# A spectral filter with a gated MLP on one core: the filtered spectrum stored class by class, its sums over twenty short rows, and a new order of work

## Chip, cores and metric

The kernel runs on one core of a Trainium2 chip. The metric is device time in microseconds (us): the median of 3 runs before the change is 196.58 us (196.56 to 196.6). Durations below are those of one profiled execution, which took 196.57 us.

## What is computed

With S = 2048 and D = 640, in bfloat16:

```
xn  = layernorm(x)                                     # over the last axis, no scale
A   = irfft2( rfft2(xn) * (w_r + i*w_i) )              # (2048, 640) real <-> (2048, 321) complex
B   = ((xn @ w_gate) * (xn @ w_up)) @ w_down           # 640 -> 1536 -> 640
out = x + A + B
```

## The kernel before

Everything is written as some 960 tasks (`T(name, engine, cost, emit, reads, writes, ...)`). Dependencies follow from the declared reads and writes. `_PLAN` is a list of (task, engine, PSUM bank) made ahead of time by a planner from the tasks' costs in ns; `replay` takes it as it stands, so it fixes the order on every engine, which of two engines does an eviction, and the bank of each product. Each engine works through its list strictly in order and waits on semaphores. A task that takes a bank waits for the last eviction of the task that had the bank before. `hold` moves the other dependencies of an eviction to its product, so that PE, not the evicting engine, waits for them.

TensorE (PE) does all products. In order of time:

- Layernorm and the gate and up products. `T0` transposes the first blocks (L814), `xt` DMAs on the queue of SP the others. `GU_f_b_w` (L973 and L951) multiplies 128 columns f of w_gate or w_up with rows b; `eG` evicts it, and `H` (L991, L993) multiplies gate with up on the Vector engine (DVE).
- The row transform: `S1` to `S5` on DVE, `R` on PE (L905), `eR` evicts. The remaining gate and up products fill PE between all these.
- The filter stage, for t = 0 to 15. `D` (L1034, 10 products each) is the last part of the forward transform over the columns: 321 frequencies in five classes of equal remainder (four classes of 64, one of 65). `eD` evicts it. `C` (L1053) is the transform over the rows. `WM` (L1070 four times, L1073 once) multiplies C in PSUM with the filter's real and imaginary parts. `SM`, after every second WM, adds and subtracts the parts over two row halves (L1086, L1087) and writes the filtered spectrum `L`. `JA`, `JB` (1024 columns each, on DVE or ACT) and `JC`, `JD` (252 columns, on GpSimd, POOL) write the mirrored or negated parts beside it. `IA` (L1116) takes five stationary blocks of 128 columns from `L`, multiplies with 64 columns of a table, and `eIA` evicts.
- The inverse over the columns, `I` (L1144) with evictions `eI` and combinations `V1` to `V5` on DVE, beside the down product `ACC` (L1221). `IV` (L1233) adds the spectral part into the same bank, `FINA` and `FIN` evict and add x, and `st_out` stores.

The evictions and copies share the helper lines L681 (ACT) and L682 (DVE and POOL). In `L` a row of 640 columns belongs to one frequency row; before the change the four classes of 64 are interleaved in it, so that for four of the five blocks of an IA the columns lie 4 elements apart, and the sums write at an odd offset:

```
o_ = 640 * (q % 4)
yl = v_l[:, lr, o_ + 128 + k:o_ + 640:4] if k < 4 else v_l[:, lr, o_:o_ + 128]
```

The filter is read from three buffers in turn (`ld_w`, on the queue of SP), one buffer for two t; further loads there are `ld_gw` (w_gate, w_up), `ld_wd` (w_down), `ld_tf`, `ld_ti`, `ld_fd`, `ld_g`, `ld_sm1` (tables) and `ld_x`.

Of the kernel before, what the change touches and what calls it, by code (L numbers as in the profile page):

```python
# [255 lines left out]
def _build_tables():  # L256
    t = {}
# [7 lines left out]
    for tt in range(16):  # L265
        for g in range(_G):
            q = tt * _G + g
# [14 lines left out]
    b = np.arange(64)  # L282
# [18 lines left out]
    l_ = 5 * np.arange(65)  # L301
    e = np.exp(-1j * two_pi * ((b[:, None] * l_[None, :]) % _D) / _D)
    w = np.where((l_ == 0) | (l_ == 320), 1.0, 2.0)[:, None] / _D * np.conj(e).T
    for o in range(2):
        own = (l_ % 2 == o).astype(np.float64)
        fd[64 * o:64 * o + 64, 512:577] = e.real * own[None, :]
        fd[64 * o:64 * o + 64, 578:641] = (e.imag * own[None, :])[:, 1:64]
        gd[63:128, 512 + 64 * o:576 + 64 * o] = w.real * own[:, None]
        gd[0:63, 512 + 64 * o:576 + 64 * o] = -(w.imag * own[:, None])[1:64]
# [59 lines left out]
_LP = 321  # L369
_YS = 1090  # L370
# [30 lines left out]
def _d_act(n):  # L401
# [4 lines left out]
    (12, 1, -1), (19, 2, -1), (10, 0, 1), (0, 3, -1), (11, 4, -1), (13, 4, -1), (18, 2, -1), (20, 2, -1), (28, 2, -1),  # L406
    (27, 2, -1), (170, 1, -1), (14, 4, -1), (8, 3, -1), (21, 1, -1), (22, 2, -1), (29, 2, -1), (23, 2, -1), (30, 1, -1),
    (31, 2, -1), (32, 2, -1), (24, 0, 3), (25, 2, -1), (26, 2, -1), (9, 0, 7), (33, 0, 1), (34, 2, -1), (35, 2, -1),
    (181, 0, 0), (182, 2, -1), (36, 1, -1), (37, 1, -1), (15, 4, -1), (43, 1, -1), (38, 1, -1), (169, 4, -1), (179, 0, 6),
    (180, 2, -1), (39, 2, -1), (40, 2, -1), (183, 2, -1), (44, 1, -1), (45, 1, -1), (46, 2, -1), (47, 2, -1), (189, 0, 1),  # L410
    (191, 0, 0), (190, 1, -1), (192, 1, -1), (193, 2, -1), (172, 4, -1), (186, 0, 6), (171, 4, -1), (112, 2, -1), (187, 1, -1),
    (41, 0, 2), (42, 1, -1), (184, 0, 7), (185, 1, -1), (16, 4, -1), (54, 2, -1), (113, 2, -1), (48, 0, 6), (49, 1, -1),
    (62, 1, -1), (194, 0, 5), (196, 0, 3), (197, 1, -1), (195, 1, -1), (188, 2, -1), (198, 2, -1), (50, 2, -1), (51, 2, -1),
    (53, 2, -1), (114, 2, -1), (55, 2, -1), (52, 2, -1), (63, 1, -1), (206, 0, 2), (207, 1, -1), (64, 1, -1), (204, 0, 7),
    (205, 1, -1), (115, 2, -1), (173, 4, -1), (209, 0, 6), (174, 4, -1), (65, 1, -1), (210, 1, -1), (66, 1, -1), (67, 2, -1),
    (56, 1, -1), (57, 2, -1), (116, 2, -1), (199, 0, 3), (200, 1, -1), (70, 2, -1), (201, 0, 2), (202, 1, -1), (203, 2, -1),
    (58, 2, -1), (208, 2, -1), (17, 4, -1), (121, 2, -1), (72, 1, -1), (1, 4, -1), (211, 0, 7), (175, 4, -1), (212, 1, -1),
    (176, 4, -1), (177, 4, -1), (73, 1, -1), (117, 0, 2), (118, 1, -1), (119, 0, 5), (74, 1, -1), (213, 2, -1), (122, 2, -1),
    (68, 2, -1), (123, 2, -1), (75, 1, -1), (76, 1, -1), (77, 2, -1), (216, 0, 1), (217, 1, -1), (214, 0, 0), (215, 1, -1),
    (218, 2, -1), (221, 0, 2), (222, 1, -1), (78, 2, -1), (124, 2, -1), (219, 0, 3), (220, 1, -1), (223, 2, -1), (80, 2, -1),  # L420
    (224, 0, 4), (120, 1, -1), (225, 1, -1), (82, 1, -1), (60, 2, -1), (226, 0, 2), (227, 1, -1), (229, 0, 6), (230, 1, -1),
    (83, 1, -1), (84, 1, -1), (178, 4, -1), (231, 0, 5), (125, 2, -1), (128, 0, 6), (126, 0, 3), (129, 1, -1), (232, 1, -1),
    (228, 2, -1), (130, 2, -1), (233, 2, -1), (131, 2, -1), (59, 4, -1), (71, 4, -1), (2, 4, -1), (236, 0, 0), (237, 1, -1),
    (61, 4, -1), (85, 1, -1), (234, 0, 2), (127, 1, -1), (86, 1, -1), (235, 1, -1), (238, 2, -1), (132, 2, -1), (92, 1, -1),
    (241, 0, 6), (242, 1, -1), (239, 0, 7), (240, 1, -1), (93, 1, -1), (243, 2, -1), (133, 2, -1), (87, 2, -1), (246, 0, 4),
    (244, 0, 1), (245, 1, -1), (94, 1, -1), (247, 1, -1), (248, 2, -1), (134, 2, -1), (69, 4, -1), (249, 0, 6), (250, 1, -1),
    (95, 1, -1), (96, 1, -1), (97, 2, -1), (251, 0, 2), (252, 1, -1), (90, 2, -1), (253, 2, -1), (88, 2, -1), (98, 2, -1),
    (100, 2, -1), (254, 0, 7), (255, 1, -1), (256, 0, 3), (257, 1, -1), (438, 4, -1), (433, 4, -1), (259, 0, 4), (260, 1, -1),
    (258, 2, -1), (137, 0, 5), (139, 0, 0), (437, 4, -1), (435, 4, -1), (441, 4, -1), (472, 4, -1), (101, 4, -1), (91, 4, -1),
    (434, 4, -1), (470, 4, -1), (3, 4, -1), (135, 0, 2), (136, 1, -1), (143, 2, -1), (138, 1, -1), (102, 1, -1), (261, 0, 7),  # L430
    (262, 1, -1), (79, 4, -1), (89, 4, -1), (141, 0, 3), (269, 0, 2), (263, 2, -1), (142, 1, -1), (140, 1, -1), (266, 0, 5),
    (267, 1, -1), (144, 2, -1), (270, 1, -1), (264, 0, 4), (265, 1, -1), (268, 2, -1), (145, 2, -1), (271, 0, 5), (274, 0, 1),
    (103, 1, -1), (104, 1, -1), (272, 1, -1), (273, 2, -1), (81, 4, -1), (442, 4, -1), (466, 4, -1), (146, 2, -1), (105, 1, -1),
    (106, 1, -1), (275, 1, -1), (279, 0, 4), (280, 1, -1), (276, 0, 0), (277, 1, -1), (278, 2, -1), (107, 2, -1), (147, 2, -1),
    (110, 2, -1), (108, 2, -1), (468, 4, -1), (469, 4, -1), (281, 0, 6), (282, 1, -1), (286, 0, 7), (287, 1, -1), (283, 2, -1),
    (284, 0, 3), (152, 0, 4), (148, 0, 6), (153, 1, -1), (99, 4, -1), (431, 4, -1), (440, 4, -1), (432, 4, -1), (4, 4, -1),
    (683, 4, -1), (109, 4, -1), (111, 4, -1), (473, 4, -1), (156, 2, -1), (429, 4, -1), (439, 4, -1), (467, 4, -1), (471, 4, -1),
    (149, 1, -1), (285, 1, -1), (288, 2, -1), (157, 2, -1), (150, 0, 0), (289, 0, 2), (151, 1, -1), (154, 0, 4), (291, 0, 6),
    (296, 0, 0), (290, 1, -1), (292, 1, -1), (155, 1, -1), (293, 2, -1), (158, 2, -1), (301, 0, 2), (299, 0, 6), (300, 1, -1),
    (294, 0, 4), (295, 1, -1), (304, 0, 7), (306, 0, 6), (6, 4, -1), (297, 1, -1), (298, 2, -1), (159, 2, -1), (160, 2, -1),  # L440
    (305, 1, -1), (307, 1, -1), (309, 0, 0), (310, 1, -1), (302, 1, -1), (303, 2, -1), (311, 0, 7), (312, 2, -1), (308, 2, -1),
    (163, 0, 5), (164, 1, -1), (167, 0, 1), (161, 0, 3), (162, 1, -1), (168, 2, -1), (314, 0, 0), (315, 2, -1), (313, 2, -1),
    (165, 0, 4), (316, 0, 6), (317, 2, -1), (166, 1, -1), (446, 0, 2), (447, 1, -1), (448, 2, -1), (474, 0, 0), (443, 0, 4),
    (444, 2, -1), (445, 1, -1), (324, 0, 7), (325, 1, -1), (477, 0, 2), (479, 1, -1), (478, 2, -1), (318, 2, -1), (321, 0, 6),
    (322, 1, -1), (436, 4, -1), (451, 0, 4), (452, 2, -1), (475, 1, -1), (476, 1, -1), (449, 0, 2), (450, 2, -1), (498, 4, -1),
    (503, 4, -1), (504, 4, -1), (497, 4, -1), (534, 4, -1), (453, 2, -1), (319, 0, 7), (320, 1, -1), (323, 2, -1), (454, 2, -1),
    (326, 0, 6), (327, 1, -1), (328, 2, -1), (505, 0, 4), (506, 1, -1), (508, 0, 0), (509, 1, -1), (510, 1, -1), (331, 0, 7),
    (332, 1, -1), (334, 0, 2), (335, 1, -1), (329, 0, 6), (507, 1, -1), (482, 0, 0), (483, 2, -1), (480, 0, 2), (481, 2, -1),
    (484, 2, -1), (455, 1, -1), (330, 1, -1), (341, 0, 7), (342, 1, -1), (336, 0, 4), (337, 1, -1), (456, 3, -1), (457, 3, -1),
    (460, 0, 5), (462, 0, 6), (463, 1, -1), (458, 0, 0), (464, 0, 7), (465, 1, -1), (461, 1, -1), (344, 0, 1), (345, 1, -1),  # L450
    (536, 0, 6), (459, 1, -1), (537, 1, -1), (339, 0, 2), (538, 1, -1), (340, 1, -1), (349, 0, 1), (532, 4, -1), (500, 4, -1),
    (499, 4, -1), (502, 4, -1), (501, 4, -1), (511, 0, 3), (333, 2, -1), (485, 2, -1), (531, 4, -1), (565, 4, -1), (535, 4, -1),
    (560, 4, -1), (530, 4, -1), (528, 4, -1), (529, 4, -1), (513, 0, 6), (351, 0, 0), (486, 2, -1), (350, 1, -1), (352, 1, -1),
    (512, 2, -1), (567, 0, 1), (568, 1, -1), (569, 1, -1), (346, 0, 5), (347, 1, -1), (487, 3, -1), (488, 3, -1), (489, 0, 4),
    (490, 1, -1), (514, 2, -1), (338, 2, -1), (515, 2, -1), (354, 0, 0), (355, 1, -1), (539, 0, 2), (540, 1, -1), (541, 1, -1),
    (493, 0, 1), (491, 0, 6), (492, 1, -1), (494, 2, -1), (356, 0, 4), (357, 1, -1), (359, 0, 7), (360, 1, -1), (517, 2, -1),
    (343, 2, -1), (516, 2, -1), (495, 0, 2), (5, 4, -1), (430, 4, -1), (533, 4, -1), (544, 0, 0), (594, 4, -1), (561, 4, -1),
# [887 lines left out]
```

## Time and profile before

| What | Value |
|---|---|
| median of 3 runs | 196.58 us |
| the profiled execution | 196.57 us, its span 194.9 us |
| granted clock of PE | 1.00 |
| WM_1 starts, WM_15 ends | 72.73 us, 125.47 us |
| SM, two instructions | 823 ns each |
| JA, JB on DVE | 452 and 517 ns; on ACT 1056 ns |
| JC, JD on POOL | 510 and 943 ns |
| an eviction eD of 64x642 | DVE 826 ns, ACT 702 ns |
| an eviction eIA of 128x320 | DVE 486 ns, ACT 440 ns |

A group line of the profile gives line, engine, operation, the names and shapes of what is written and read, and a count; then busy time in us and the mean of one in ns; then the engine's idle time ahead of it and what ended most of it. PE is the matmuls, PEld the loading of their stationary operand, which overlaps them. Neighbouring instructions of an engine overlap a little, so their durations add up to more than the time they take. The chain is followed back from the last instruction.

### The profile page before, as it was taken

Reading aid. Unit: us, or ns where it says so; the run is one execution under the profiler, and the core shown is the slowest. Engines: PE = TensorE matmul, PEld = TensorE weight load, DVE = VectorE, ACT = ScalarE, POOL = GpSimd, SP = SyncE. Lnnn points to the kernel's source line nnn. Section 1 sums busy time; section 2 is a strip of 40 time slices with the busy share of each in tenths; the row PEclk is TensorE's granted clock in tenths of the full one; section 3 lists DMA queues with packets and bytes.
Section 4 is the critical chain, followed back from the end, with each engine's and each line's share of the span. In section 5 each row is a group of like instructions: output and inputs, shape, how many; then the busy total and the mean of one; then the engine's idle time right before and its main releaser. Section 6 shows DMA issues by size and latency. Waiting matters only on the chain.

```text
span 194.9 us, 4074 instructions
## 1 busy us (share of the span) xinstructions
PE 190.9 (98%) x1568; PEld 120.5 (62%) x1568; DVE 176.7 (91%) x369; ACT 136.4 (70%) x275; POOL 12.2 (6%) x22
## 2 busy tenths in 40 slices
PE   8899999999999999999999999999999999999995
PEld 8797454454454565555655555557777777777774
DVE  3899999999999999999989999987999999999713
ACT  3899999999884679989999999667305523253130
POOL 1000000000000000331031221120000000000000
DMA  5999974016869921366465510005001543135412
GB/s 173 324 370 324 214 98 111 0 37 105 155 130 222 258 68 27 96 145 193 118 153 135 153 36 31 3 0 170 4 0 53 144 143 104 40 95 172 134 68 67
DMA packets 29666, 23.73 MB, mean 122 GB/s; under 512 B 10448, under 2 KB 27600, under 8 KB 29520
## 3 DMA queue, kind: packets, MB, share of 16 engines
q1 hardware_dynamic: 28848, 23.08, 46.5%
q10 hardware_dynamic: 800, 0.41, 0.7%
q8 instruction: 12, 0.20, 0.5%
q14 instruction: 6, 0.05, 0.1%
HBM read 18.89 MB, written 2.62 MB: 110 GB/s over the span
## 4 chain that ended last, share of the span: by engine, by line
PE 95%; DVE 2%; DMA 1%; ACT 1%; issue 0%
PE ps L951 48%; PE ps L1221 27%; PE ps L973 5%; PE ps L1116 3%; PE ps L1034 2%; PE ps L1053 2%; PE ps L905 2%; PE ps L1144 2%; PE ps L1233 2%; DMA arena<-in_A_x_dram 1%; DVE arena L754 1%; PE ps L814 1%; ACT arena L681 1%; DVE arena L682 0%; DVE arena L761 0%
## 5 line engine op out<-in xcount | busy, mean ns | idle before, releaser
L681 ACT ACTIVATE arena<-ps 128x512 bf16<-128x512 f32 (+5 forms) x211 | 111.3, 582 | 48.8 <-PE ps L1233 13.8
L951 PE MATMUL ps<-arena 128*128 128x512 bf16 x440 | 101.9, 379 | 0.0
L951 PEld LDWEIGHTS ps<-arena 128*128 128x128 bf16 x440 | 40.9, 98 | 43.1 <-ACT arena L681 0.9
L1221 PE MATMUL ps<-arena 128*128 128x320 bf16 (+2 forms) x396 | 57.2, 295 | 0.0
L1221 PEld LDWEIGHTS ps<-arena 128*128 128x128 bf16 x396 | 37.6, 98 | 13.2
L1070 DVE TENSOR_TENSOR arena<-ps,arena 128x256 bf16<-128x256 f32 x64 | 22.6, 414 | 1.5 <-PE ps L1053 1.3
L991 DVE TENSOR_TENSOR arena<-arena 128x512 bf16<-128x512 bf16 x44 | 18.7, 426 | 0.6 <-ACT arena L681 0.2
L1260 DVE TENSOR_TENSOR arena<-arena 128x640 bf16<-128x640 bf16 x15 | 7.0, 486 | 5.4 <-ACT arena L681 5.4
L682 DVE CAST arena<-ps 128x512 bf16<-128x512 f32 (+4 forms) x16 | 10.1, 639 | 1.5 <-PE ps L973 0.4
L745 ACT ACTIVATE arena<-arena 128x640 bf16<-128x640 bf16 x12 | 10.2, 849 | 0.1
L682 POOL COPY arena<-arena 64x252 bf16<-64x252 bf16 x8 | 4.1, 510 | 92.8 <-DVE arena L1087 92.5
L973 PE MATMUL ps<-arena 128*128 128x128 bf16 (+1 forms) x120 | 9.5, 237 | 0.3 <-DVE arena L682 0.3
L1116 PEld LDWEIGHTS ps<-arena 128*128 128x128 bf16 x160 | 7.9, 116 | 3.0
L736 ACT ACTIVATE arena<-arena 128x640 bf16<-128x640 bf16 x12 | 9.0, 753 | 0.2
L973 PEld LDWEIGHTS ps<-arena 128*128 128x128 bf16 x120 | 8.4, 98 | 1.1 <-issue 0.4
L1100 POOL TENSOR_SCALAR arena<-arena 64x252 bf16<-64x252 bf16 x8 | 7.5, 943 | 22.9 <-DVE arena L1087 22.6
L1116 PE MATMUL ps<-arena 128*128 128x64 bf16 x160 | 8.3, 198 | 0.0
L1233 PE MATMUL ps<-arena 128*128 128x320 bf16 (+2 forms) x33 | 8.3, 295 | 0.0
L1034 PEld LDWEIGHTS ps<-arena 128*128 128x128 bf16 x160 | 6.4, 98 | 2.7 <-issue 0.5
L857 DVE TENSOR_TENSOR arena<-arena 128x768 f32<-128x768 bf16 (+1 forms) x10 | 7.9, 789 | 0.0
L1073 DVE TENSOR_TENSOR arena<-ps,arena 128x260 bf16<-128x260 f32 x16 | 6.9, 432 | 0.0
L1034 PE MATMUL ps<-arena 128*128 128x64 bf16 (+1 forms) x160 | 6.9, 193 | 0.0
(61 smaller groups left out, 184.3 us busy)
## 6 DMA issues: line engine op xcount, KB each, us to landing
arena<-in_A_x_dram SPq DMA_DIRECT2D x19, 160.0 KB, 2.6
arena<-in_A_w_i_dram SPq DMA_DIRECT2D x30, 80.2 KB, 2.3
arena<-in_A_w_r_dram SPq DMA_DIRECT2D x30, 80.2 KB, 2.3
out_dram<-arena SPq DMA_DIRECT2D x15, 160.0 KB, 1.9
arena<-in_B_w_gate_dram SPq DMA_DIRECT2D x4, 320.0 KB, 6.5
arena<-in_A_x_dram SPq DMA_DIRECT2D x1, 1280.0 KB, 10.8
arena<-c_tf SPq DMA_DIRECT2D x4, 256.0 KB, 4.6
arena<-c_ti SPq DMA_DIRECT2D x2, 512.0 KB, 5.0
```

The costliest lines, as they stand in the source:

```text
L681: return c.e.activation(dst, src, _ACTF.Copy)
L682: return c.e.tensor_copy(dst, src)
L736: return c.e.activation(v_jk, v_x[:, b, :], _ACTF.Copy, scale=1.0 / _D, accum_out=v_m32[:, b:b + 1])
L745: return c.e.activation(v_jk, v_x[:, b, :], _ACTF.Square, scale=-1.0, bias=v_m32[:, b:b + 1], accum_out=v_ss[:, b:b + 1])
L951: ins = c.e.matmul(ps[:, bk, :], v_gw[:, w, j, ft, :], v_xt[:, j, rows], start=(j == 0), stop=(j == 4))
L973: ins = c.e.matmul(ps[:, bk, i * n:(i + 1) * n], v_gw[:, w, j, ft0 + i, :], v_xt[:, j, rows], start=(j == 0), stop=(j == 4))
L991: return c.e.tensor_tensor(v_ht[:, ft0, rows], gb[:, 0, :], gb[:, 1, :], _OP.mult)
L1034: ins = c.e.matmul(ps[:, bk + i, k * 64:k * 64 + n], v_uq[:, k, t + i, :], v_fd[:, k * 128 + w * n: k * 128 + w * n + n], start=True, stop ...
L1070: c.e.tensor_tensor(dst, xh, wv, _OP.mult)
L1116: ins = c.e.matmul(ps[:, bk, 64 * k:64 * k + 64], yl, v_ti[:, q, 0, :], start=True, stop=True)
L1221: ins = c.e.matmul(ps[:, bk, 0:sl3.stop - sl3.start], v_ht[:, ft, a * 128:(a + 1) * 128], v_wd[:, ft, sl3], start=(ft == _FT_ORDER[0]), st ...
L1233: return c.e.matmul(ps[:, bank_of(own), 0:sl3.stop - sl3.start], v_sm[:, 2, :], v_v[:, a, sl3], start=False, stop=True)
```

## The change

The spectrum `L` and the products `PR` ahead of it are stored class by class: block b of a row is the class of 65 (b = 0) or one of the four of 64, and a block is 128 columns in `L` and 66 in `PR`. All five stationary blocks of an IA are contiguous then. WM runs over the classes outside and their members inside: it reads PSUM contiguously, where it had read in steps of 64, and the filter in steps of 10, where it had read four neighbours at a time. SM works on twenty rows of 66 instead of one run of 1284 elements written as four rows of 321. A memset on POOL (`pad`) zeroes what is beyond a class's members. In JC and JD the destination moves behind the source (at 65), and the table `g` has its rows in the new order.

```diff
-        gd[63:128, 512 + 64 * o:576 + 64 * o] = w.real * own[:, None]
-        gd[0:63, 512 + 64 * o:576 + 64 * o] = -(w.imag * own[:, None])[1:64]
+        gd[0:65, 512 + 64 * o:576 + 64 * o] = w.real * own[:, None]
+        gd[65:128, 512 + 64 * o:576 + 64 * o] = -(w.imag * own[:, None])[1:64]
...
+_LB = 66
...
-        b_pr = alloc("PR", 8 * 321)
-        b_l = alloc("L", 2 * 2624)
+        b_pr = alloc("PR", 8 * 5 * _LB)
+        b_l = alloc("L", 2 * 2560)
...
-        v_pr = V("PR").rearrange("p (w g n) -> p w g n", w=2, g=4)
-        v_l = V("L").rearrange("p (r n) -> p r n", r=2)
+        v_pr = V("PR").rearrange("p (w g b c) -> p w g b c", w=2, g=4, b=5)
+        v_l = V("L").rearrange("p (r g b c) -> p r g b c", r=2, g=4, b=5)
...
-                        xh = ps[:, bk:bk + 2, 0:256].rearrange("p g (k h m) -> p h g m k", k=4, h=2)[:, h]
-                        wv = wt[:, w, :, 0:320].rearrange("p g (m k) -> p g m k", k=10)
-                        wv = wv[:, :, :, 1:5] if h == 0 else wv[:, :, :, 9:5:-1]
-                        dst = v_pr[:, w, 2 * pb:2 * pb + 2, 65:321].rearrange("p g (h m k) -> p h g m k", h=2, k=4)[:, h]
+                        xh = ps[:, bk:bk + 2, 0:256].rearrange("p g (k h m) -> p h g k m", k=4, h=2)[:, h]
+                        wv = wt[:, w, :, 0:320].rearrange("p g (m k) -> p g k m", k=10)
+                        wv = wv[:, :, 1:5] if h == 0 else wv[:, :, 9:5:-1]
+                        dst = v_pr[:, w, 2 * pb:2 * pb + 2, 1:5, 32 * h:32 * h + 32]
...
-                d5 = v_pr[:, :, 2 * pb:2 * pb + 2, 0:65]
+                d5 = v_pr[:, :, 2 * pb:2 * pb + 2, 0, 0:65]
...
-            wm = T("WM_%d" % t, "dve", 1792.0, em_wm,
+            if t == 0:
+                def em_pad(c):
+                    return c.e.memset(v_pr[:].rearrange("p w g b c -> p (w g b) c")[:, :, 64:_LB], 0.0)
+                T("pad", "pool", 300.0, em_pad, writes=[(b_pr, None)], prio=pq - 0.002)
+            wm = T("WM_%d" % t, "dve", 1710.0, em_wm,
...
-                pa_, pb_ = v_pr[:, 0], v_pr[:, 1]
-                l_ = v_l[:, lr, 63:2623].rearrange("p (g n) -> p g n", g=4)[:, :, 0:321]
+                pa_, pb_ = (v_pr[:, w].rearrange("p g b c -> p (g b) c") for w in range(2))
+                l_ = v_l[:, lr].rearrange("p g b c -> p (g b) c")[:, :, 0:_LB]
                 c.e.tensor_tensor(l_[0:64], pa_[0:64], pb_[64:128], _OP.subtract)
                 return c.e.tensor_tensor(l_[64:128], pa_[64:128], pb_[0:64], _OP.add)
-            T("SM_%d" % t, "dve", 1900.0, em_sm, reads=[(b_pr, ("r", 0, 2))],
+            T("SM_%d" % t, "dve", 1640.0, em_sm, reads=[(b_pr, ("r", 0, 2))],
...
-                src = l0[:, :, 1:64] if five else l0[:, :, 65:321]
-                dst = l1[:, :, 0:63] if five else l0[:, :, 321:577]
+                src = v_l[:, lr, :, 0, 1:64] if five else v_l[:, lr, :, 1:5, 0:64]
+                dst = v_l[:, lr, :, 0, 65:128] if five else v_l[:, lr, :, 1:5, 64:128]
...
-{"act": 1200.0, "dve": 460.0, "pool": 1300.0},
+{"act": 1000.0, "dve": 440.0, "pool": 1000.0 if neg else 560.0},
...
-                        yl = v_l[:, lr, o_ + 128 + k:o_ + 640:4] if k < 4 else v_l[:, lr, o_:o_ + 128]
+                        yl = v_l[:, lr, q % 4, (k + 1) % 5]
...
-                ia = T("IA_%d" % q, "pe", 173.0, em_ia,
+                ia = T("IA_%d" % q, "pe", 146.0, em_ia,
```

`_PLAN` is replaced as a whole. The tasks are the same but for `pad`. From ACT to DVE go eR_13, eG_3_8_0, eD_2_0_0, JB_1, eIA_5, eIA_8, eD_10_0_0, JB_7, eIA_22, JA_13, eIA_30 and eI_2; from DVE to ACT eG_0_8_1, eR_15, eD_2_1_0, eIA_6, JA_7, eG_3_12_0, eG_10_12_1, JB_15 and eIA_28. DVE's queue from WM_1 to WM_9, before and after:

```
before: WM_1 WM_0 SM_1 H_2_8 JA_1 H_3_8 WM_3 WM_2 SM_3 H_4_8 JA_3 JB_3 WM_4 WM_5 H_5_8 SM_5 eIA_6
        JB_5 H_6_8 JA_5 WM_6 WM_7 H_7_8 SM_7 JA_7 H_8_8 WM_9
after:  WM_1 WM_0 SM_1 H_1_8 JA_1 JB_1 WM_2 WM_3 H_2_8 SM_3 JA_3 JB_3 H_3_8 WM_4 WM_5 H_4_8 H_5_8 SM_5
        eIA_5 H_6_8 JB_5 JA_5 WM_6 WM_7 eIA_8 H_7_8 SM_7 eD_10_0_0 JB_7 H_8_8 WM_9
```

On PE, GU, D, C and IA change places by a few positions (IA_13 goes ahead of D_12_1, for one), and in the column stage the parts of ACC and IV do. D_12_1 takes the banks of C_9 in the new order, which WM_9 frees, and GU_8_12_1 one that WM_15 frees. On the queue of SP the loads ahead of 120 us are shuffled: ld_sm1 goes ahead of ld_x5, ld_gw6_1 behind ld_gw8_0, the transpose xt8 from place 32 to 40, ld_w2_0_0 and ld_w2_0_2 from 36 and 37 to 54 and 55, ld_wd7 from 44 to 79. On POOL some of the mirrors swap.

## Prediction

> **What bounds the kernel now.** I read the page's engine shares and chain first, then the groups by form, the waits, and the Vector engine's time line between 72 and 126 us.
>
> ```profile
> PE 190.9 (98%) x1568; PEld 120.5 (62%) x1568; DVE 176.7 (91%) x369; ACT 136.4 (70%) x275; POOL 12.2 (6%) x22
> ...
> PE 95%; DVE 2%; DMA 1%; ACT 1%; issue 0%
> ```
>
> TensorE is busy for 98% of the span and is 95% of the chain that ended last: whatever shortens or stops PE moves the end by as much. DVE at 91% is close behind. The stretches show where the two meet (columns: length, busy us of PE, PEld, DVE, ACT, POOL, clock, DMA share, GB/s):
>
> ```profile
> 72.70:104.20 31.50, 31.50 (x281) 17.36 (x280) 30.29 (x74) 29.84 (x53) 5.98 (x8) 1.00 0.49 125
> 104.20:125.50 21.30, 21.26 (x189) 11.78 (x187) 20.08 (x47) 20.40 (x39) 4.35 (x6) 1.00 0.24 65
> ```
>
> This is the filter stage, from WM_1 to WM_15. PE never stops, and DVE idles for only 1.2 of each 31.5 or 21.3 us. Part of that is 0.03 us between dependent instructions; the rest is waiting for the products C:
>
> ```profile
> DVE arena L1070 <- PE ps L1053: 1.3, 4, 0.4
> ```
>
> So DVE has little more than 1.3 us in hand over 53 us.
>
> **The weights of the inverse column products (IA, L1116), on PE.** The groups by form (busy us, mean ns):
>
> ```profile
> L1116 PE MATMUL ps<-arena 128*128 128x64 bf16 x160 | 8.3, 198 | 0.0
> L1116 PEld LDWEIGHTS ps<-arena 128*128 128x128 bf16 x160 | 7.9, 116 | 3.0
> L1034 PEld LDWEIGHTS ps<-arena 128*128 128x128 bf16 x160 | 6.4, 98 | 2.7 <-issue 0.5 <-ACT arena L681 0.2
> L1034 PE MATMUL ps<-arena 128*128 128x64 bf16 x128 | 6.5, 193 | 0.0
> ```
>
> and their pace in the chain (start, us, what):
>
> ```profile
> 69.05 0.89 PE ps L1034 x30
> ...
> 81.64 0.67 PE ps L1116 x20
> ```
>
> L1034 has the same shape with contiguous stationary columns: 0.89/30 = 29.7 ns each. L1116, of whose five weights four step by 4 elements, takes 0.67/20 = 33.5. Five at 29.5 are 147 ns instead of 168, and 32 groups save 32 x 21 = 0.66 us. A rule speaks against this: the Trainium skill, "TensorE: Matmul & The Clock Gate", section "Weight-path perf modes — Fast Weight Load (FWL) and DoubleRow", has 128 bf16 weights loaded fast from chunks that are packed or strided alike. By it the saving is 0. The rows differ by 18 ns per load and 4 ns of pace, so I take 0.66 and keep 0 for a rival.
>
> **The sums SM (L1086, L1087), on DVE.** 20 rows of 66 are 1320 elements instead of 1284. The same operation took 426 ns for 512 elements (L991) and 823 for 1284: 0.51 ns per element, so 36 more cost 19 ns, twice per SM, 0.3 us over eight. The Trainium skill, "VectorE: DVE Perf Modes", section "Mode 2×_1P — pack two bf16 into one 32-bit read", asks for 4-byte aligned operands. The old sums write at an odd element offset, so by that rule they ran one element a cycle and the aligned layout would save about 0.6 us in each of 16 instructions, 10 us of DVE. The 0.51 ns rate is already two per cycle, so I count no gain. What short rows cost at this rate no row shows: 0 to another 0.6 us per instruction if two per cycle were lost.
>
> **The weighting WM (L1070), on DVE.** The same 256 elements, now reading PSUM contiguously and the filter in steps of 10:
>
> ```profile
> L1070 DVE TENSOR_TENSOR arena<-ps,arena 128x256 bf16<-128x256 f32 x64 | 22.6, 414 | 1.5 <-PE ps L1053 1.3
> L1073 DVE TENSOR_TENSOR arena<-ps,arena 128x260 bf16<-128x260 f32 x16 | 6.9, 432 | 0.0
> L1242 DVE TENSOR_TENSOR arena<-ps,arena 128x320 bf16<-128x320 f32 x1 | 0.5, 492 | 0.6 <-PE ps L1233 0.6
> L1242 DVE TENSOR_TENSOR arena<-ps,arena 128x192 bf16<-128x192 f32 x1 | 0.4, 359 | 0.5 <-PE ps L1233 0.5
> ```
>
> Contiguous PSUM and contiguous second operand interpolate to 426 ns at 256 elements, so the strided read of 414 pays nothing that could be won back. L1073 already steps through the filter by 5 and lies 14 ns above what 256 elements would give it. I take 0; the bounds are -12 and +14 ns for each of 64, or -0.8 to +0.9 us.
>
> **Mirrors, pad, table.** JA and JB keep 1024 elements (452 and 517 ns on DVE, 1056 on ACT): 0, within 0.05 us each. JC and JD keep 252 on POOL, which is 6% busy; after SM_1 they have about 0.5 us before IA_3, and beyond that PE waits. The new memset has 80 elements: between the 97 ns of POOL's smallest memset and the 294 of its 128-element select. It can run once S5_4 is done (65.5 us) and is needed by WM_1 at 72.7; were it late, WM_1 would be late by as much. The inverse table keeps its shape. Zero for each.
>
> **The new order.** *Queue of SP.* Filter loads move among the transposes; the runs they need land 3 us or more ahead of their WM in the old trace, and where ld_w2 now queues behind ld_w4 (which waits for the last R, near 67.7) it lands near 72.3 for a WM at 77. xt8 lands near 59, needed at 63.3. ld_wd7 moves past 35 issues to near 90, with its use after 131. Only ld_gw6_1 becomes thin: behind the 0.65 MB of ld_gw8_0 it lands near 22.6 instead of 20.8, and PE asks at 22.7. I take 0, at most 0.2. ld_sm1 ahead of ld_x5 ends PE's 0.2 us wait for c_sm and delays sm8 on ACT by 0.2: even. *POOL* swaps mirrors only.
>
> *DVE.* Here I count. From the start of WM_1 to the end of WM_9 the new queue holds, beyond the old: H_1_8 (0.43), JB_1 (0.52), an inverse eviction eIA_8 (0.49), a forward eviction eD_10_0_0 (0.83), JB_7 for JA_7 (0.07), and 4 x 0.04 for the sums: 2.5 us, some 2.3 after the 0.08 us by which neighbours overlap. WM_1 cannot move: it follows C_1, which has the same work ahead of it on PE. The old stretch:
>
> ```profile
> 72.73 1.41 DVE L1070 TENSOR_TENSOR arena<-ps,arena 128x256 bf16<-128x256 f32 x4
> ...
> 100.74 1.42 DVE L1070 TENSOR_TENSOR arena<-ps,arena 128x256 bf16<-128x256 f32 x4 [0.42 <-PE ps L1053]
> 102.07 0.45 DVE L1073 TENSOR_TENSOR arena<-ps,arena 128x260 bf16<-128x260 f32 x1
> ```
>
> WM_9 ends at 102.52 with 0.62 us of waits before it (0.20 and this 0.42). With every wait refilled it ends at 102.5 - 0.6 + 2.3 = 104.2. D_12_1 takes the banks that WM_9 frees. It started at 103.3; 13 cheaper IA ahead of it (-0.27) and one more of them (+0.15) put it at 103.2. PE therefore stands at least 1.0 to 1.1 us. At WM_15 the count is alike, not added: 2.8 us more work, 1.5 us of waits, so 125.5 becomes 126.8, against GU_8_12_1 at 126.35 - 28 x 0.021 = 125.8: again 1.0. PE has no idle time later to take this back in. ACT gains some 3 us of room in the stage (six evictions and mirrors fewer, one eviction more), which shortens nothing: no PE wait there ends on ACT. The column stage follows, where IV_8_0 at 168.7 follows V5_8 by only 0.1 us; it also slips with PE, and DVE's further 0.2 us of waits and its 1 us wait before V1_0 can be refilled: nothing more.
>
> **Sum.** Against this execution's 196.57 us (span 194.9 and 1.67 around it, 0.01 below the median of 196.58): -0.66 for the weights, +1.05 for DVE if it never waits, +0.2 for waits that remain when C and WM take turns: +0.6, or 197.2 us.
>
> **Rivals.** *DVE keeps up (faster).* The mechanism is the handover WM_9 to D_12_1: if DVE does the stretch 1 us quicker than the rows add up to, PE never stands and 0.66 stays: 195.9. The deciding point for faster by over 0.2% (0.39 us, about what a measurement of this kernel can tell from no change) is a stall below 0.27 us, that is 45 WM instructions each about 18 ns shorter. For it: the diff's own cost of a WM falls from 1792 to 1710 and of an SM from 1900 to 1640. Against it: SM took 1.65 before, and the contiguous rows above leave 12 ns at best. *The weights save nothing:* 168 ns stays, the stall does too: 197.9. *Strided filter reads cost 14 ns:* 0.5 us more at WM_9, 0.9 at WM_15: 197.9. *Short rows end two per cycle:* 0.6 us x 16 on a full DVE: about 206.
>
> **Chances.** DVE-bound with 0.66 saved: 0.60 (own range 196.6 to 197.9, of which 0.15 falls within 0.2%). DVE keeps up: 0.22 (0.17 faster, 0.05 within). Strided filter 0.08, no saving 0.05, short rows 0.05, all slower. Faster 0.17, within 0.20, slower 0.63. The range 196.0 to 198.3 leaves out the short rows and the best of the second case.
>
> **What would show it.** Right: L1116's successor at 29.5 ns pace and 98 ns loads; PE gaps at D and GU ended by the weighting's last line, first near 103 us; DVE's waits for C mostly gone; SM near 842 ns, WM's parts near 414. Wrong: PE unbroken from 72 to 131 us; or WM parts below 400; or gaps placed in the column stage instead.

## Result: 6.6% slower, and DVE now sets the filter stage

The changed kernel takes 209.59 us (median of 5 runs, 209.4 to 209.75) against 196.59 for the kernel before on the same chip: a ratio of 1.0663, 95% interval 1.0647 to 1.0678. The profiled execution has a span of 208.0 us at a granted clock of 1.00. The prediction was 197.2 us, with a range that ended at 198.3.

The engine line and the chain's shares, from the page of the changed kernel:

```profile
PE 192.3 (92%) x1551; PEld 119.5 (57%) x1568; DVE 190.5 (92%) x372; ACT 136.5 (66%) x272; POOL 12.5 (6%) x23
...
PE 62%; DVE 34%; issue 2%; DMA 2%; SPq 0%; ACT 0%; DVEq 0%
```

PE had 95% of the chain and has 62%. DVE went from 2% to 34%, and its busy time rose by 13.8 us, about what the kernel lost. The groups by form show where (line numbers are one to five higher than before):

```profile
L1071 DVE TENSOR_TENSOR arena<-ps,arena 128x256 bf16<-128x256 f32 x64 | 34.9, 611 | 0.1
L1118 PE MATMUL ps<-arena 128*128 128x64 bf16 x160 | 8.3, 193 | 4.0 <-DVE arena L1074 3.6 <-POOL arena L683 0.3
L1074 DVE TENSOR_TENSOR arena<-ps,arena 128x260 bf16<-128x260 f32 x16 | 7.0, 440 | 0.0
L1118 PEld LDWEIGHTS ps<-arena 128*128 128x128 bf16 x160 | 6.8, 98 | 8.3 <-DVE arena L1074 4.9 <-issue 0.9 <-ACT arena L1102 0.4
L1091 DVE TENSOR_TENSOR arena<-arena 64x1320 bf16<-64x1320 bf16 x8 | 6.7, 842 | 0.3
L1092 DVE TENSOR_TENSOR arena<-arena 64x1320 bf16<-64x1320 bf16 x8 | 6.7, 840 | 0.1
```

The four parts of WM (L1071) take 611 ns each instead of 414. The loads of IA (L1118) fell from 116 to 98 ns and the sums came to 842, both as forecast. DVE idles 0.1 us ahead of all 64 parts; PE waits for WM's last line instead. These are the stretches from WM_1 to the end of WM_9 and from there to WM_15 (length; busy us of PE, PEld, DVE, ACT, POOL; clock; DMA share; GB/s), and three of PE's waits (us in total, times, longest):

```profile
73.12:111.18 38.06, 31.87 (x268) 16.59 (x271) 37.38 (x73) 28.94 (x51) 5.80 (x8) 1.00 0.44 117
111.18:139.42 28.24, 23.49 (x204) 12.47 (x207) 27.71 (x53) 20.80 (x38) 4.58 (x6) 1.00 0.25 68
```

```profile
PE ps L1118 <- DVE arena L1074: 3.6, 5, 1.0
PE ps L952 <- DVE arena L1074: 3.4, 5, 1.0
PE ps L1035 <- DVE arena L1074: 2.4, 3, 0.9
```

The handover from WM_9 to D_12_1 (PE's time line: start, us; in brackets the idle time ahead and what ended it):

```profile
111.23 0.47 PE L1035 MATMUL ps<-arena 128*128 128x64 bf16 x10 [0.85 <-DVE arena L1074]
```

PE is idle for some 10.9 of these 66.3 us (a few matmul records are missing in the trace, so it is rather less); most of that ended with WM's last line (the three rows make 9.4). Before, PE was idle for 0.04 of 52.8. The sum closes on the stage. The parts of WM follow each other every 523 ns instead of 332, and 64 x 191 ns are 12.2 us. The new order's added DVE work, 2.8 us by the prediction's count (some 2.6 by the runs below), brings it to 15.0. The 1.5 us of DVE waits that were in the stage are gone: 13.5. WM_15 ends at 139.42 instead of 125.47, 13.95 later, and the stage began 0.39 later: 13.56. The end of the span moved by 13.2.

### The profile page after: what moved, and what is told of

It is laid out like the page before. It is cut to its first block, busy times and chain, and to the rows that moved or that the text cites. A ratio compares the mean times of both kernels' runs of the same rounds, so it can differ in the third digit from the quotient of the medians.

```text
span 208.0 us, 4065 instructions
## 1 busy us (share of the span) xinstructions
PE 192.3 (92%) x1551; PEld 119.5 (57%) x1568; DVE 190.5 (92%) x372; ACT 136.5 (66%) x272; POOL 12.5 (6%) x23
## 4 chain that ended last, share of the span: by engine, by line
PE 62%; DVE 34%; issue 2%; DMA 2%; SPq 0%; ACT 0%; DVEq 0%
PE ps L1223 25%; PE ps L952 25%; DVE arena L1071 16%; PE ps L974 4%; DVE arena L683 4%; DVE arena L992 3%; DVE arena L1092 3%; DVE arena L1091 3%; DVE arena L1074 3%; PE ps L906 2%; PE ps L1146 2%; PE ps L1235 2%; DMA arena<-in_A_x_dram 2%; DVE arena L1103 1%; PE ps L815 1%
## 5 line engine op out<-in xcount | busy, mean ns | idle before, releaser
L952 PE MATMUL ps<-arena 128*128 128x512 bf16 x423 | 99.4, 379 | 4.2 <-DVE arena L1074 3.4
L952 PEld LDWEIGHTS ps<-arena 128*128 128x128 bf16 x440 | 40.9, 98 | 47.3 <-DVE arena L1074 4.3
L1223 PEld LDWEIGHTS ps<-arena 128*128 128x128 bf16 x396 | 37.7, 98 | 13.3
L1071 DVE TENSOR_TENSOR arena<-ps,arena 128x256 bf16<-128x256 f32 x64 | 34.9, 611 | 0.1
L683 DVE CAST arena<-ps 128x320 bf16<-128x320 f32 (+4 forms) x17 | 10.4, 626 | 2.9 <-PE ps L1118 1.3
L1118 PE MATMUL ps<-arena 128*128 128x64 bf16 x160 | 8.3, 193 | 4.0 <-DVE arena L1074 3.6
L1118 PEld LDWEIGHTS ps<-arena 128*128 128x128 bf16 x160 | 6.8, 98 | 8.3 <-DVE arena L1074 4.9
L1035 PEld LDWEIGHTS ps<-arena 128*128 128x128 bf16 x160 | 6.2, 98 | 4.9 <-DVE arena L1074 3.2
L974 PEld LDWEIGHTS ps<-arena 128*128 128x128 bf16 x120 | 8.4, 98 | 1.0 <-issue 0.2
L1054 PE MATMUL ps<-arena 128*128 128x321 bf16 x32 | 6.5, 299 | 1.0 <-DVE arena L1092 0.6
```

Source lines behind the costliest of these rows:

```text
L683: return c.e.tensor_copy(dst, src)
L952: ins = c.e.matmul(ps[:, bk, :], v_gw[:, w, j, ft, :], v_xt[:, j, rows], start=(j == 0), stop=(j == 4))
L974: ins = c.e.matmul(ps[:, bk, i * n:(i + 1) * n], v_gw[:, w, j, ft0 + i, :], v_xt[:, j, rows], start=(j == 0), stop=(j == 4))
L1035: ins = c.e.matmul(ps[:, bk + i, k * 64:k * 64 + n], v_uq[:, k, t + i, :], v_fd[:, k * 128 + w * n: k * 128 + w * n + n], start=True, stop ...
L1071: c.e.tensor_tensor(dst, xh, wv, _OP.mult)
L1118: ins = c.e.matmul(ps[:, bk, 64 * k:64 * k + 64], yl, v_ti[:, q, 0, :], start=True, stop=True)
```

## Experiments

The question left by the profile is why a part of WM costs 197 ns more: it reads PSUM another way, reads the filter in steps of 20 bytes, and writes runs of 32 elements. A second question is what the other parts of the change were worth. Two theories were set against each other first: (1) the steps in which the filter is read, (2) the way the results are stored. Unless another is given, the time before, on the same chip, was 196.58 us for the first four runs and 196.54 for the others.

**The old loop on the new layout.** Members outside, the four classes inside: the filter is read four neighbours at a time again, and the results scatter into the classes, 66 elements (132 bytes) apart.

```diff
-  xh = ps[...].rearrange("p g (k h m) -> p h g k m", k=4, h=2)[:, h]
-  wv = wt[:, w, :, 0:320].rearrange("p g (m k) -> p g k m", k=10)
-  wv = wv[:, :, 1:5] if h == 0 else wv[:, :, 9:5:-1]
-  dst = v_pr[:, w, 2 * pb:2 * pb + 2, 1:5, 32 * h:32 * h + 32]
+  xh = ps[...].rearrange("p g (k h m) -> p h g m k", k=4, h=2)[:, h]
+  wv = wt[:, w, :, 0:320].rearrange("p g (m k) -> p g m k", k=10)
+  wv = wv[:, :, :, 1:5] if h == 0 else wv[:, :, :, 9:5:-1]
+  dst = v_pr[:, w, 2 * pb:2 * pb + 2, 1:5, 32 * h:32 * h + 32].rearrange("p g k m -> p g m k")
```

> The changed kernel with one thing back: WM runs over the members outside and the classes inside, so it reads four neighbouring filter elements and PSUM in steps of 64, as before, and scatters its result into the class-by-class PR (steps of 66). Theory 1 (the filter read in steps of 10 elements, 20 bytes, is what made WM's parts 611 ns): they return to about 414 ns, and what is left is the prediction's own sum, 197.2 us (196.6 to 197.9), with PE held up near 103 us by WM_9. Theory 2 (storing into short class rows costs it): they stay near 600 ns or more, and the time near 209 us.

It took 256.98 us, a ratio of 1.2991 (1.2926 to 1.3056). Its groups:

```profile
L1071 DVE TENSOR_TENSOR arena<-ps,arena 128x256 bf16<-128x256 f32 x64 | 75.5, 1461 | 5.7 <-PE ps L1054 5.7
L1074 DVE TENSOR_TENSOR arena<-ps,arena 128x260 bf16<-128x260 f32 x16 | 10.1, 631 | 0.0
```

That is far beyond what either theory had expected (414 ns, or near 600 and more). The PSUM reads and the filter reads are those of the kernel before, whose parts took 414 ns, so what is left for the 1461 ns are the scattered stores. Reading the filter by neighbours does not help when the results have to go to separate classes. This run could not tell theory 1 from 2, because it brought in a larger cost of its own. PE's granted clock was 0.926 in this profile, in which PE was busy for 81% of the span.

The same loop under the order of before gave the same, so the order has no part in it:

> The class-by-class layout with WM's old loops, under the old order: the contiguous weights and the longer sums alone. Theory 1: WM's parts at 414 ns, L1118's pace 29.5 ns, SM 842 ns, DVE's waits for C take up the 0.3 us of the sums, and the time is 195.9 to 196.1 us, faster than before. If scattered stores cost DVE (theory 2), slower than 200 us.

256.26 us, 1.3014 (1.2969 to 1.3058), the parts at 1463 ns.

**The new order alone, with the code of before.** Only `_PLAN` is exchanged (without `pad`).

> The new order alone on the kernel before (old layout, old loops, no memset). The prediction's count of DVE's queue says that PE stands about 1 us by WM_9 and no more later, and without the cheaper weights that is 197.6 to 197.8 us. Rival (the new order is harmless, DVE refills its waits and more): 196.6 us.

197.09 us, 1.0027 (1.0015 to 1.0039): 0.5 us slower. DVE's group, and the two places in the stage where PE's loads waited for WM's last line:

```profile
L1070 DVE TENSOR_TENSOR arena<-ps,arena 128x256 bf16<-128x256 f32 x64 | 22.5, 411 | 0.1
```

```profile
98.17 0.41 PEld L1116 LDWEIGHTS ps<-arena 128*128 128x128 bf16 x10 [0.23 <-DVE arena L1073]
104.13 0.35 PEld L1034 LDWEIGHTS ps<-arena 128*128 128x128 bf16 x10 [0.17 <-DVE arena L1073]
```

DVE's waits ahead of WM fell from 1.5 to 0.1 us. WM_9 ends at 104.07 and D_12_1 starts at 104.13, and WM_15 ends at 126.89; the prediction had counted 104.2 and 126.8. But WM_1 begins at 73.00 here and at 72.73 before, so that the stretch to the end of WM_9 grew by 1.3 us, where the count has 1.7, and the one to WM_15 by 1.15. What the count made of it at the end was too much: 0.5 us came out.

**The new layout alone, under the order of before.** The new `pad` stands right behind S5_4.

> The new layout and loops under the old order (the memset put behind S5_4). WM's parts stay near 611 ns. 64 parts x 0.19 us of pace are 12 us on DVE, less its 1.3 us of waits, less 0.66 us on PE: 206.5 to 208 us if the loops are nearly all of the loss and the new order adds 1 to 2 us to it; 202 us or less if the new order is what made DVE's longer parts fall on PE.

207.16 us, 1.0537 (1.0518 to 1.0555), WM's parts at 606 ns. So the layout with its loops costs 10.6 us, and the new order 2.4 more on top, though alone it costs 0.5. Most of the difference is DVE's waits. Under the new layout DVE has none left in either order (0.1 us ahead of WM's parts in both), so that the added work comes out in full: from WM_1 the stretch to WM_9's end takes 36.17 us here and 38.06 in the changed kernel, 1.9 more, and the one to WM_15's end 63.70 and 66.30, 2.6 more, beside a count of 2.3 and 2.8. With the old layout the same order made it 1.3 and 1.15.

**The filter read as runs.** Everything of the change stays, but for the addresses at which WM's four parts read the filter: one run of 128 elements.

```diff
-  wv = wt[:, w, :, 0:320].rearrange("p g (m k) -> p g k m", k=10)
-  wv = wv[:, :, 1:5] if h == 0 else wv[:, :, 9:5:-1]
+  wv = wt[:, w, :, 128 * h:128 * h + 128].rearrange("p g (k m) -> p g k m", k=4)
```

> The changed kernel, but the four parts of WM read the filter as one run of 128 elements instead of in steps of 10: the loops, the PSUM reading, the class-by-class result, the short rows and the new order stay, and the elements of the filter are the wrong ones. Theory 1 (the step of the filter's reads is the whole of the loss): WM's parts fall from 611 to 405-425 ns, and the kernel to about 196.6 us: 196.6 before, -0.66 for the weights, +0.5 for the new order as measured with the old layout, +0.2 for the longer sums; at most the 197.2 of the prediction. Theory 2 (the writing in short runs of 32, rows of 66 apart, costs as well): parts at 480-611 ns and 200-209 us.

```profile
L1070 DVE TENSOR_TENSOR arena<-ps,arena 128x256 bf16<-128x256 f32 x64 | 22.5, 411 | 0.1
L1117 PEld LDWEIGHTS ps<-arena 128*128 128x128 bf16 x160 | 6.8, 98 | 3.5 <-ACT arena L1101 0.4 <-issue 0.3 <-DVE arena L1073 0.3
```

The parts are back at 411 ns, and the kernel at 197.24 us, 1.0033 (1.0021 to 1.0045). That settles theory 1: some 12.3 of the lost 13.0 us come from the step in which the filter is read, and none from the short runs written or from PSUM read in order.

Under the order of before:

> The same reading of the filter as runs, under the order of before (the new memset right behind S5_4). Theory 1: WM's parts at 405-425 ns, no stop of PE in the filter stage, L1118 at 98 ns loads and 29.5 ns pace, and 195.9-196.1 us: the 0.66 us of the weights come out as time. Theory 2 (writing): parts at 480-611 ns, 200-207 us. Rival on the weights (DVE's 0.3 us of longer sums takes it): 196.4-196.6.

196.24 us, 0.9988 (0.9981 to 0.9994), the parts at 414 ns: 0.3 us faster than before, where 0.45 to 0.65 were expected.

**Contiguous weights alone.** The kernel before; IA takes its five blocks as runs of 128 columns.

```diff
-  yl = v_l[:, lr, o_ + 128 + k:o_ + 640:4] if k < 4 else v_l[:, lr, o_:o_ + 128]
+  yl = v_l[:, lr, o_ + 128 * k:o_ + 128 * k + 128]
```

> The kernel before, with one edit: IA takes its five stationary blocks as runs of 128 columns instead of in steps of 4, so it multiplies the wrong columns. Layout, sums and order are those of before. Theory 1: loads 116 to 98 ns, pace 33.5 to 29.5, and 32 groups of 5 save 0.66 us: 195.9 us. Rival (the load hides behind the matmul before it, or DVE's waits for C take the time): 196.4-196.6.

196.29 us, 0.9986 (0.998 to 0.9993). The same 20 products in the chain that took 0.67 us before (start, us, what):

```profile
81.71 0.58 PE ps L1116 x20
```

That is 29 ns each instead of 33.5. Over the 32 groups, the time from one task's start to the next falls by 0.65 us, as forecast. Yet 0.25 us reach the end. Between the first L1034 and the first L1221 of the stage, 0.38 are saved (62.45 to 62.07 us). Much of the rest is given back where PE waits for evictions on ACT. One such place, before and then with contiguous weights (start, us; a gate or up product, and the loads of the C behind it with their idle time):

```profile
107.78 1.24 PE L951 MATMUL ps<-arena 128*128 128x512 bf16 x5
108.85 0.11 PEld L1053 LDWEIGHTS ps<-arena 128*128 128x128 bf16 x2 [0.32 <-ACT arena L681]
```

```profile
107.63 1.24 PE L951 MATMUL ps<-arena 128*128 128x512 bf16 x5
108.83 0.11 PEld L1053 LDWEIGHTS ps<-arena 128*128 128x128 bf16 x2 [0.46 <-ACT arena L681]
```

PE comes to the product 0.15 us earlier and to C 0.02 earlier. In both traces the load starts 0.05 us behind the end of an eviction of 128x512 on ACT, which came 0.02 us earlier than before. Both traces hold the same 1568 loads in the same order, so PE's lead can be followed load by load: some 0.7 us are gathered in the stage (0.65 by the tasks' starts), and 0.33 lost again in four jumps, of 0.09 us (93.8, a GU), 0.04 (100.2), 0.14 (108.85) and 0.07 (114.9, the last three at C). The waits at 93.8 and 108.85 end on ACT; for the other two the trace names no engine. PE had entered the stage 0.07 us later than before, and 0.06 go at the first I (132.0), again without a name: 0.24 are left at the end of the span.

**A sweep of steps.** One kernel, in which each WM_t reads or writes its four parts in another way; only durations are read.

> The new layout under the old order; each WM_t reads or writes its four parts in another way (t 0 and 14: filter in steps of 10, 1: 1, 2: 2, 3: 4, 4: 16, 5: 5, 6: 6, 7: 7, 8: 12, 9: 8, 10: 9; 11: filter as runs, PSUM in steps of 4; 12: the old loop, filter in steps of 10 in the inner loop of four, result contiguous; 13 and 15: filter as runs, result in steps of 4 and of 8). Elements are permuted, so the output is another. Only the durations per part are read. Theory A (two reads out of each 16 bytes are needed): steps 1, 2, 4 at 414 ns, 5 to 7 between, 8 to 16 alike at 600-611. Theory B (any reads 16 bytes apart or less are free): 1 to 8 at 414, 9 to 16 at 611. Theory C (cost by the number of bytes swept): rising evenly from 414 at 1 past 611 at 10 to about 740 at 16. PSUM in steps of 4: 414-420 by the old kernel's steps of 64 (a penalty would show as 500 and more). t 12: 414. Result in steps of 4: 414 if writes behave as reads of four bytes apart, 600-1450 if each 2-byte write far from its neighbour pays; steps of 8: the same or more, towards the 1461 of the steps of 66.

Here are the four parts of single WM (stretch; length, busy us of the four; clock, DMA share, GB/s), in this order: filter in steps of 1, 10, 4, 5, 6, 7, 8 and 12 elements; PSUM in steps of 4; result in steps of 4; the loop and steps of before; result in steps of 8.

```profile
72.97:74.35 1.38, 1.38 (x4) 1.00 0.00 0
74.65:76.85 2.20, 2.18 (x4) 1.00 0.00 0
80.36:81.77 1.41, 1.40 (x4) 1.00 0.61 159
89.53:91.05 1.52, 1.51 (x4) 1.00 0.89 303
95.66:97.40 1.74, 1.73 (x4) 1.00 0.70 190
97.67:99.65 1.98, 1.96 (x4) 1.00 0.03 6
102.97:105.16 2.19, 2.18 (x4) 1.00 0.79 201
105.44:107.60 2.16, 2.15 (x4) 1.00 0.52 139
111.25:112.66 1.41, 1.40 (x4) 1.00 0.74 179
119.23:121.71 2.48, 2.48 (x4) 1.00 0.49 132
121.96:123.37 1.41, 1.40 (x4) 1.00 0.00 0
129.24:133.40 4.16, 4.16 (x4) 1.00 0.00 0
```

From one part's start to the next, in ns:

| filter's step, elements of 2 bytes | 1, 2, 4 | 5 | 6 | 7 | 8 | 9, 10, 12, 16 |
|---|---|---|---|---|---|---|
| mean pace | 332 | 357 | 416 | 472 | 526 | 517 to 531 |

Theory A, two reads out of each 16 bytes, fits. Up to 8 bytes apart a read costs nothing, between 10 and 16 bytes the price rises, and from 16 bytes on it stands still. Theory B (free up to 16 bytes) and C (by the bytes swept) are out. The full price is some 190 ns for 256 reads, 0.75 ns a read. DMA traffic has no part in it (the second row has none), nor has the reversed order of the classes in half of WM's parts: the sweep's steps of 10 run forwards and are as slow, 527 ns against 523. PSUM in steps of 4 costs nothing, nor does the old loop, which has the filter's step of 10 only between runs of four. Stores are stricter: in steps of 8 bytes the pace behind the first part is 599 ns, 1.0 ns an element more than contiguous, and in steps of 16 bytes 1140, or 3.2. The 132 bytes of the first experiment, at 1143, cost no more than the 16.

## Why the prediction was wrong

- **WM: the step that failed.** "I take 0; the bounds are -12 and +14 ns for each of 64." It measured +197 ns in duration and +191 in pace: 12.2 us on an engine that the prediction had itself shown to be full; with the filter read as runs, 12.3 us came back. The bound was drawn from L1073, which reads the filter in steps of 5, as if 10 were more of the same. The sweep shows that 5 lies just at the foot of the slope (357 against 332) and 10 on top of it (527). The 14 ns by which L1073 lay above its size may have been the first sign of that slope (no run reads L1073's filter in one run), and were read as its upper end. The rival of strided filter reads was of this kind, but priced with the same 14 ns.
- **A rule of the Trainium skill that was not weighed** spoke against this step. "SBUF — State Buffer", in the section on the DMA port swizzle, has a box on cachelines: 16 bytes long, with at least two hits on each needed for full bandwidth. The filter is read 20 bytes apart, one hit per line. The runs agree with the two hits: 8 bytes apart free, 16 bytes apart the full price. The same box goes on to call 8 bf16 the free distance; here steps of 8 elements made the pace 526 ns against 332, so of the two statements the measurement backs the first. The page gives no price; 0.75 ns per read is this case's.
- **The weights: half right.** Pace 29 ns and loads 98 came as said, and 0.65 us of PE's time with them; by the rule that strided weights load as fast, it would have been 0. But the sum took all of it as time, and alone it brought 0.25. The cover was missed. "No PE wait there ends on ACT" holds for the matmuls, but not for the loads ahead of them: in the kernel before, those of C already waited 0.5 us for ACT. ACT kept its times to 0.02 us, and C started when it did although PE came earlier. In the new order the saving hides wholly: D_12_1 starts at 104.12 with contiguous weights and at 104.13 without, since WM_9 sets it.
- **DVE's count in the new order: its times met in part by luck, its price too dear.** WM_9's end (104.07 for 104.2) and WM_15's (126.89 for 126.8) were met by the order alone. But WM_1, which "cannot move", began 0.27 us late, and the work added was some 0.4 us less than counted. The prediction puts +1.25 us on the order without the weights (its 197.9), though 0.27 of the stop at D_12_1 was there only because cheaper weights brought PE to it earlier. The run shows waits of 0.23 and 0.17 us for WM's last line, and +0.5 in all.
- **The rest of the sum agrees by luck.** With the filter as runs, what is left of the change takes 197.24 us, beside a forecast of 197.2. The total agrees, its parts do not: -0.25 for the weights and +0.5 for the order, each measured alone, make +0.25, and both together with the longer sums made +0.7, no better than the order alone. In this order, where DVE sets the stage, PE's saving is worth nothing.
- **SM: right.** 842 ns for 842. The rate of 0.51 ns an element, which the prediction took for two per cycle, is half of the 1.04 ns that its two rows of L1242 give (359 ns for 192 elements, 492 for 320). It is kept on twenty short rows, and was there before at the odd offset at which the alignment rule would have lost it.
- **Mirrors, pad, table: right** as far as can be seen: with the filter as runs and the old order nothing is lost to them (196.24 us, against 196.29 for the weights alone). In the changed kernel PE waited once, at 81.75 us, 0.26 us for a mirror on POOL.
- **Signs named.** "PE gaps at D and GU ended by the weighting's last line" is what the trace shows, though at IA as well, from 84 us on instead of 103, and ten times as much. Rivals: DVE did not keep up; the weights saved PE time; the rows did not fall back to one element a cycle.

Of the versions that compute the whole, none beat the kernel before; the two that took 0.3 us less read other columns or other elements of the filter. A filter put into class order ahead of WM, by POOL for instance, could reach for these 0.3 us; it was not tried.

## What to carry to other kernels

A layout is paid for on both sides: before making one operand contiguous for its reader, list what each instruction on the way now reads and writes in steps, in bytes, and price each step by its own row or a short sweep, never by extending a smaller step. The cost of a step is not proportional: in DVE's reads here it was nothing up to 8 bytes, then a slope, then flat. And a saving on an engine counts only where that engine sets the stage; when the neighbour has 1.3 us in hand over 53, a cost of 0.2 us per instruction there decides everything.

## Unexpected in the hardware

All of these are from products of float32 in PSUM with 2-byte elements in SBUF, 256 per partition.

- DVE's reads of 2-byte elements from SBUF: free at steps of 2 to 8 bytes, 0.1 ns a read more at 10, 0.33 at 12, 0.55 at 14, and 0.72 to 0.78 from 16 to 32 bytes.
- DVE's writes of 2-byte elements: 1.0 ns an element more at steps of 8 bytes, 3.2 at 16 and at 132. A scattered store cost four times a stepped read.
- DVE's reads of float32 from PSUM in steps of 16 bytes (pace 332 ns) or 256 (333, in the kernel before) cost no more than contiguous ones (332, with the filter as runs).
- The 65-long fifth part of WM slowed down with its neighbours' stores: 631 ns behind parts that store 132 bytes apart, against 432. Its own accesses were the same. The four parts do not show their whole cost in the time to the next start: the first is followed after 920 ns, the others after some 1140. The 220 ns that the first lacks and the 200 that the fifth is longer would fit stores that lag behind the instruction that makes them; no run tests this.
